# One load queue for all gate and up weights, a longer warm-up, and a new written-out order in a fused spectral and gated-linear kernel

## The chip, the cores and the metric

The kernel runs on one core of one Trainium2 chip. The metric is the device time of one execution in microseconds (us). A core has TensorE (PE, matmuls into PSUM), VectorE (DVE), ScalarE (ACT), GpSimd (POOL) and SyncE (SP, which only issues DMAs here). They run side by side and wait for each other through semaphores.

## The reference, cut to what matters

```python
def _layernorm(x, axis=-1, eps=1e-5):
    m = jnp.mean(x, axis=axis, keepdims=True)
    v = jnp.var(x, axis=axis, keepdims=True)
    return (x - m) / jnp.sqrt(v + eps)

def _A_ref(x, w_r, w_i):                      # x (1, 2048, 640)
    X = rfft2(x.astype(float32), axes=(-2, -1))
    X = X * (w_r + 1j * w_i)                  # w (2048, 321)
    return irfft2(X, s=(S, D), axes=(-2, -1)).astype(bfloat16)

def _B_ref(x, w_gate, w_up, w_down):
    g = jnp.einsum("bsd,df->bsf", x, w_gate)  # w_gate, w_up (640, 1536)
    u = jnp.einsum("bsd,df->bsf", x, w_up)
    return jnp.einsum("bsf,fd->bsd", g * u, w_down)   # w_down (1536, 640)

x = A_x
xn = _layernorm(x, axis=-1)
return x + _A_ref(xn, A_w_r, A_w_i) + _B_ref(xn, B_w_gate, B_w_up, B_w_down)
```

## The kernel before

The 2048 rows of x are split into 16 blocks of 128 rows. A block is normalised in place in SBUF, and then used by two branches that both end in the same PSUM accumulation.

The **gated branch** needs the block transposed. For blocks 0 to 3 PE transposes it (task `T0_b`, L809) and ACT or DVE copies it out of PSUM (`eT0_b`; for blocks 0 and 1 in two halves, `_act` with two of five column groups and `_dve` with three, L827). For blocks 4 to 15 SP issues a DMA transpose (`xtb`, L803), which waits for the block's normalisation. The matmuls of gate and up are the tasks `GU_f_b_u`: f is the first of twelve slabs of 128 hidden columns, b the first row block, u is 0 for gate and 1 for up. A task for four row blocks is five matmuls with 512 columns (L949, the matmul on L952); one for fewer blocks covers two slabs with ten matmuls (L969, the matmul on L974). Copies `eG` bring the results to SBUF and DVE multiplies them (`H`, L990). The down projection is the tasks `ACC_a_h_k` (L1218) per row block a, half h of the columns and group of slabs from k.

The **spectral branch** runs as a DFT by pieces: sums and differences on DVE (`S1_g` to `S5_g` per group of blocks, L854 to L895), matmuls `R_b` per block (L898) with copies `eR_b`, then `D`, `C`, the multiplication by the spectral weights (`WM`, `SM`, with copies `JA` to `JD`), and the way back (`IA`, `I`, `V1` to `V5`, and `IV`, which adds into the accumulation of the down projection). `FIN` adds x and the result is stored.

**Layer norm** of a block: either `bn` (two, L755), `ag` on DVE, or two ACT passes `sm` and `sq` (L737, L746); then `sd` (square root, ACT, L770), `rs` (reciprocal, DVE, L779) and `mul` (subtract and scale, DVE, L794). Groups of blocks share `sd` and `rs`: `sd_4` and `rs_4` serve blocks 4 and 5, `sd_5` and `rs_5` blocks 6 and 7. Blocks 0, 1, 4 and 5 use `bn`, the others ACT.

Every engine runs its tasks strictly in an order written out in `_PLAN` (L405): a tuple of task number, engine (0 PE, 1 ACT, 2 DVE, 3 POOL, 4 SP) and PSUM bank. `replay` (L151) walks the plan and `compute_waits` (L196) derives the semaphore waits from what each task reads, writes and frees; a task waits for all of these, and everything after it on its engine waits too. The durations given to tasks in the code are the planner's own; on the chip only the order, the engine, the bank and the waits of a plan count.

Loads go out as DMAs in the same way. SP issues nearly all; before, `ld_x0b` and `ld_gw0_1` go out on ACT. A load `ld_gwf_u` brings slabs from f on (two of them, 320 KB; four for f = 8, 640 KB) of gate or up (L921 to L926); `ld_xi` are pieces of x (`ld_x0a`, `ld_x0b` 80 KB each, `ld_x1` to `ld_x3` one block of 160 KB, `ld_x4` four blocks, `ld_x5` eight); `ld_sm1`, `ld_fd`, `ld_tf`, `ld_ti`, `ld_g` are DFT tables; `ld_w` spectral weights; `ld_wd` the down weights; `ld_xr` x again for the final sum. The first DVE pass over x is `S1_0`, which also waits for `mul3`; `R_0` and `R_1` need `S5_0`, and `S5_4` is what `R_12` to `R_15` need.

At the start, PE runs a **warm-up**: matmuls of ones with ones, whose result nobody reads (L712 to L719), 40 of them with 128 columns, and later a **filler** of six with 64 columns (L701 to L709), after the first transposes.

Of the kernel before, what the change touches and what calls it, by code (L numbers as in the profile page):

```python
# [400 lines left out]
def _d_act(n):  # L401
# [4 lines left out]
    (11, 4, -1), (10, 0, 5), (18, 2, -1), (12, 1, -1), (19, 2, -1), (20, 2, -1), (8, 3, -1), (0, 3, -1), (13, 4, -1),  # L406
    (28, 2, -1), (27, 2, -1), (14, 4, -1), (169, 4, -1), (15, 4, -1), (170, 1, -1), (21, 1, -1), (36, 1, -1), (22, 2, -1),
    (29, 2, -1), (30, 1, -1), (171, 4, -1), (172, 4, -1), (23, 2, -1), (24, 0, 0), (9, 0, 2), (37, 1, -1), (25, 1, -1),
    (38, 1, -1), (31, 2, -1), (32, 2, -1), (33, 0, 3), (26, 2, -1), (179, 0, 5), (39, 2, -1), (34, 2, -1), (40, 2, -1),
    (35, 2, -1), (43, 1, -1), (44, 1, -1), (45, 1, -1), (46, 2, -1), (47, 2, -1), (181, 0, 1), (182, 1, -1), (180, 1, -1),  # L410
    (183, 2, -1), (112, 2, -1), (41, 0, 7), (42, 1, -1), (189, 0, 6), (191, 0, 2), (184, 0, 0), (192, 1, -1), (190, 1, -1),
    (193, 2, -1), (48, 0, 4), (16, 4, -1), (186, 0, 1), (51, 2, -1), (50, 2, -1), (49, 1, -1), (185, 1, -1), (187, 1, -1),
    (188, 2, -1), (52, 2, -1), (54, 2, -1), (113, 2, -1), (53, 2, -1), (62, 1, -1), (63, 1, -1), (194, 0, 7), (64, 1, -1),
    (196, 0, 6), (174, 4, -1), (173, 4, -1), (55, 2, -1), (197, 1, -1), (195, 1, -1), (198, 2, -1), (114, 2, -1), (65, 1, -1),
    (204, 0, 0), (206, 0, 5), (56, 1, -1), (115, 2, -1), (57, 2, -1), (58, 2, -1), (116, 2, -1), (201, 0, 3), (205, 1, -1),
    (202, 1, -1), (66, 1, -1), (207, 1, -1), (199, 0, 2), (200, 1, -1), (208, 2, -1), (203, 2, -1), (67, 2, -1), (70, 2, -1),
    (211, 0, 1), (212, 1, -1), (17, 4, -1), (1, 4, -1), (72, 1, -1), (209, 0, 4), (117, 0, 0), (210, 1, -1), (118, 1, -1),
    (73, 1, -1), (74, 1, -1), (119, 0, 2), (121, 2, -1), (176, 4, -1), (221, 0, 7), (178, 4, -1), (175, 4, -1), (213, 2, -1),
    (216, 0, 5), (120, 1, -1), (217, 1, -1), (122, 2, -1), (68, 2, -1), (123, 2, -1), (75, 1, -1), (214, 0, 1), (215, 1, -1),
    (218, 2, -1), (124, 2, -1), (82, 1, -1), (76, 1, -1), (77, 2, -1), (125, 2, -1), (78, 2, -1), (71, 4, -1), (177, 4, -1),  # L420
    (59, 4, -1), (219, 0, 6), (60, 2, -1), (80, 2, -1), (226, 0, 4), (222, 1, -1), (220, 1, -1), (223, 2, -1), (224, 0, 0),
    (227, 1, -1), (225, 1, -1), (228, 2, -1), (130, 2, -1), (229, 0, 1), (230, 1, -1), (126, 0, 6), (127, 1, -1), (83, 1, -1),
    (128, 0, 2), (129, 1, -1), (231, 0, 0), (232, 1, -1), (233, 2, -1), (131, 2, -1), (236, 0, 4), (467, 4, -1), (237, 1, -1),
    (84, 1, -1), (85, 1, -1), (92, 1, -1), (234, 0, 5), (235, 1, -1), (238, 2, -1), (469, 4, -1), (69, 4, -1), (432, 4, -1),
    (3, 4, -1), (61, 4, -1), (86, 1, -1), (436, 4, -1), (87, 2, -1), (132, 2, -1), (241, 0, 7), (242, 1, -1), (93, 1, -1),
    (94, 1, -1), (246, 0, 2), (4, 4, -1), (431, 4, -1), (81, 4, -1), (239, 0, 3), (440, 4, -1), (240, 1, -1), (243, 2, -1),
    (244, 0, 4), (245, 1, -1), (247, 1, -1), (249, 0, 5), (251, 0, 0), (95, 1, -1), (96, 1, -1), (252, 1, -1), (250, 1, -1),
    (254, 0, 3), (255, 1, -1), (256, 0, 2), (257, 1, -1), (133, 2, -1), (248, 2, -1), (261, 0, 7), (134, 2, -1), (139, 0, 5),
    (135, 0, 0), (141, 0, 3), (97, 2, -1), (88, 2, -1), (90, 2, -1), (253, 2, -1), (266, 0, 2), (140, 1, -1), (262, 1, -1),
    (468, 4, -1), (437, 4, -1), (438, 4, -1), (472, 4, -1), (470, 4, -1), (100, 2, -1), (98, 2, -1), (258, 2, -1), (143, 2, -1),  # L430
    (142, 1, -1), (137, 0, 6), (138, 1, -1), (259, 0, 5), (260, 1, -1), (263, 2, -1), (144, 2, -1), (102, 1, -1), (267, 1, -1),
    (136, 1, -1), (264, 0, 6), (265, 1, -1), (268, 2, -1), (145, 2, -1), (269, 0, 5), (103, 1, -1), (270, 1, -1), (276, 0, 7),
    (277, 1, -1), (104, 1, -1), (271, 0, 1), (272, 1, -1), (273, 2, -1), (146, 2, -1), (274, 0, 0), (105, 1, -1), (275, 1, -1),
    (106, 1, -1), (147, 2, -1), (107, 2, -1), (281, 0, 3), (282, 1, -1), (279, 0, 7), (280, 1, -1), (284, 0, 0), (285, 1, -1),
    (286, 0, 2), (152, 0, 0), (153, 1, -1), (278, 2, -1), (473, 4, -1), (108, 2, -1), (435, 4, -1), (434, 4, -1), (466, 4, -1),
    (442, 4, -1), (439, 4, -1), (2, 4, -1), (91, 4, -1), (99, 4, -1), (154, 0, 6), (155, 1, -1), (89, 4, -1), (441, 4, -1),
    (79, 4, -1), (101, 4, -1), (110, 2, -1), (283, 2, -1), (156, 2, -1), (148, 0, 3), (149, 1, -1), (287, 1, -1), (289, 0, 5),
    (288, 2, -1), (157, 2, -1), (294, 0, 0), (295, 1, -1), (150, 0, 6), (291, 0, 1), (292, 1, -1), (290, 1, -1), (293, 2, -1),
    (296, 0, 4), (151, 1, -1), (297, 1, -1), (298, 2, -1), (301, 0, 0), (299, 0, 2), (309, 0, 1), (471, 4, -1), (109, 4, -1),
    (111, 4, -1), (433, 4, -1), (302, 1, -1), (300, 1, -1), (158, 2, -1), (7, 4, -1), (310, 1, -1), (311, 0, 3), (304, 0, 4),  # L440
    (306, 0, 5), (312, 1, -1), (307, 1, -1), (305, 1, -1), (303, 2, -1), (314, 0, 0), (159, 2, -1), (160, 2, -1), (161, 0, 1),
    (163, 0, 6), (162, 1, -1), (167, 0, 4), (168, 1, -1), (315, 2, -1), (164, 2, -1), (308, 2, -1), (313, 2, -1), (316, 0, 3),
    (317, 2, -1), (318, 2, -1), (165, 0, 6), (504, 4, -1), (502, 4, -1), (501, 4, -1), (500, 4, -1), (166, 1, -1), (321, 0, 5),
    (322, 1, -1), (443, 0, 6), (445, 2, -1), (444, 1, -1), (477, 0, 0), (446, 0, 3), (447, 1, -1), (448, 2, -1), (479, 1, -1),
    (324, 0, 2), (325, 1, -1), (478, 2, -1), (474, 0, 5), (475, 1, -1), (476, 1, -1), (449, 0, 3), (319, 0, 7), (320, 1, -1),
    (450, 2, -1), (451, 0, 1), (452, 2, -1), (453, 2, -1), (456, 3, -1), (457, 3, -1), (323, 2, -1), (455, 2, -1), (326, 0, 0),
    (327, 1, -1), (508, 0, 3), (510, 1, -1), (509, 1, -1), (331, 0, 5), (332, 1, -1), (341, 0, 7), (342, 1, -1), (505, 0, 3),
    (507, 1, -1), (506, 1, -1), (329, 0, 0), (454, 1, -1), (330, 1, -1), (482, 0, 1), (483, 2, -1), (480, 0, 5), (334, 0, 7),
    (481, 2, -1), (335, 1, -1), (349, 0, 4), (429, 4, -1), (462, 0, 3), (463, 1, -1), (536, 0, 0), (538, 1, -1), (537, 1, -1),
    (344, 0, 2), (460, 0, 3), (458, 0, 5), (350, 1, -1), (459, 1, -1), (345, 1, -1), (464, 0, 6), (465, 1, -1), (461, 1, -1),  # L450
    (336, 0, 7), (337, 1, -1), (339, 0, 0), (340, 1, -1), (328, 2, -1), (484, 2, -1), (486, 2, -1), (485, 2, -1), (503, 4, -1),
    (498, 4, -1), (497, 4, -1), (533, 4, -1), (531, 4, -1), (530, 4, -1), (499, 4, -1), (513, 0, 5), (511, 0, 3), (567, 0, 1),
    (569, 1, -1), (568, 1, -1), (346, 0, 7), (351, 0, 0), (514, 2, -1), (539, 0, 5), (512, 2, -1), (333, 2, -1), (515, 2, -1),
    (517, 2, -1), (516, 2, -1), (560, 4, -1), (487, 3, -1), (488, 3, -1), (347, 1, -1), (683, 4, -1), (528, 4, -1), (495, 0, 2),
    (541, 1, -1), (496, 1, -1), (540, 1, -1), (489, 0, 7), (490, 2, -1), (352, 1, -1), (359, 0, 1), (360, 1, -1), (493, 0, 3),
    (491, 0, 2), (492, 1, -1), (354, 0, 4), (355, 1, -1), (356, 0, 6), (494, 1, -1), (357, 1, -1), (534, 4, -1), (5, 4, -1),
    (561, 4, -1), (532, 4, -1), (535, 4, -1), (529, 4, -1), (542, 0, 1), (543, 2, -1), (366, 0, 0), (544, 0, 6), (545, 2, -1),
    (592, 4, -1), (564, 4, -1), (518, 3, -1), (565, 4, -1), (591, 4, -1), (596, 4, -1), (559, 4, -1), (563, 4, -1), (430, 4, -1),
    (601, 0, 4), (519, 3, -1), (367, 1, -1), (602, 1, -1), (603, 1, -1), (361, 0, 3), (362, 1, -1), (522, 0, 2), (523, 1, -1),
# [62 lines left out]
def _build(nc, A_x, A_w_r, A_w_i, B_w_gate, B_w_up, B_w_down, out, opts=None):  # L522
# [3 lines left out]
    with es:  # L526
# [170 lines left out]
        T("eps", "pool", 150.0, em_eps, writes=[(b_ve, None)], prio=-1.0)  # L697
        fills = []
        nfill = opts.get("nfill", 6)

        def em_fill(c):  # L701
            bk = bank_of(c.t)
            ins = None
# [642 lines left out]
```

## Time and profile before

| | |
|---|---|
| median of 3 runs | 199.5 us (198.73 to 199.68) |
| the profiled execution's own time | 199.59 us |
| its span, first to last instruction | 197.9 us |
| mean granted TensorE clock | 0.991 |
| PE busy | 192.2 us, 97% of the span |
| DVE busy | 175.4 us, 89% |
| ACT busy | 137.9 us, 70% |
| longest waits of DVE for a load of x, of PE for a gate load | 3.1 us; 0.6 us |

The span is what the profiler saw of the program; the execution's own time has 1.7 us more around it. Times in the views are counted from the start of the span. A wait in brackets is time in which the engine stood idle before an instruction, with what released it. One plan task is several instructions of a view: T0 is on L816, GU on L974 or L952, the copies on L681 (ACT) and L682 (DVE), all plain loads on L675 and DMA transposes on L804, since helpers issue them. Matmuls overlap in the views: one begins before the one before it has ended.

### The profile page before, as it was taken

The page shows a single profiled execution, that of the slowest core. Times are in us where ns is not written, and L with a number is a line of the kernel's source. Part 1 is how long each engine was busy: PE and PEld are TensorE (multiplying, and loading weights), DVE is VectorE, ACT ScalarE, POOL GpSimd, SP SyncE. Part 2 cuts the span into 40 slices and gives each one's busy share as a digit, 9 for nine tenths or more (in the row PEclk, how much of TensorE's full clock was granted, in tenths as well). Part 3 has the DMA queues.
Part 4 walks back from the last instruction along what each step waited for, and adds up shares of the span by engine and source line. Part 5 has one row for each costly group of instructions (what it writes and reads, how often), then busy time and mean ns, then how long its engine had stood idle before and what let it go on. Part 6 is the DMA issues. An engine that isn't in the chain of part 4 may idle for free.

```text
span 197.9 us, 4118 instructions
## 1 busy us (share of the span) xinstructions
PE 192.2 (97%) x1587; PEld 123.4 (62%) x1587; DVE 175.4 (89%) x364; ACT 137.9 (70%) x280; POOL 13.1 (7%) x22
## 2 busy tenths in 40 slices
PE   8699989999999999999999999999999999999995
PEld 8598735454454465556555555558677777777764
DVE  3588999999999989999999999985999999999843
ACT  3879998998976479998899998967504541440340
POOL 1000000000000000320330320330000000000000
PEclk9889999999999999999999999999999999999999
DMA  6999364979412016238492524004101252034242
GB/s 176 332 372 319 50 167 105 190 156 123 96 33 70 3 46 180 68 94 259 127 247 60 151 65 136 0 0 137 65 3 61 74 165 79 34 122 134 71 162 66
DMA packets 29666, 23.73 MB, mean 120 GB/s; under 512 B 10448, under 2 KB 27600, under 8 KB 29520
## 3 DMA queue, kind: packets, MB, share of 16 engines
q1 hardware_dynamic: 28848, 23.08, 43.8%
q10 hardware_dynamic: 800, 0.41, 0.7%
q8 instruction: 12, 0.20, 0.4%
q14 instruction: 6, 0.05, 0.1%
HBM read 18.89 MB, written 2.62 MB: 109 GB/s over the span
## 4 chain that ended last, share of the span: by engine, by line
PE 84%; DMA 7%; DVE 4%; ACT 3%; SPq 1%; issue 0%
PE ps L952 44%; PE ps L1222 25%; PE ps L1117 3%; PE ps L1035 2%; DMA arena<-in_B_w_gate_dram 2%; DMA arena<-in_B_w_down_dram 2%; PE ps L1054 2%; PE ps L1234 2%; PE ps L974 2%; DMA arena<-in_A_x_dram 2%; PE ps L906 2%; PE ps L1145 1%; ACT arena L738 1%; ACT arena L681 1%; DVE arena L797 1%; PE ps L816 1%
## 5 line engine op out<-in xcount | busy, mean ns | idle before, releaser
L681 ACT ACTIVATE arena<-ps 128x512 bf16<-128x512 f32 (+6 forms) x217 | 113.3, 579 | 50.8 <-PE ps L1234 18.0
L952 PE MATMUL ps<-arena 128*128 128x512 bf16 x420 | 97.4, 379 | 0.6 <-DMA arena<-in_B_w_gate_dram 0.6
L952 PEld LDWEIGHTS ps<-arena 128*128 128x128 bf16 x420 | 38.9, 98 | 42.1 <-DMA arena<-in_B_w_gate_dram 1.1
L1222 PE MATMUL ps<-arena 128*128 128x320 bf16 (+2 forms) x396 | 57.1, 295 | 0.2 <-DMA arena<-in_B_w_down_dram 0.2
L1222 PEld LDWEIGHTS ps<-arena 128*128 128x128 bf16 x396 | 37.4, 98 | 13.8 <-issue 0.5
L1071 DVE TENSOR_TENSOR arena<-ps,arena 128x256 bf16<-128x256 f32 x64 | 22.6, 415 | 1.9 <-PE ps L1054 1.8
L992 DVE TENSOR_TENSOR arena<-arena 128x512 bf16<-128x512 bf16 x42 | 17.9, 433 | 1.2 <-ACT arena L681 0.5
L974 PE MATMUL ps<-arena 128*128 128x128 bf16 (+1 forms) x160 | 15.3, 262 | 0.0
L974 PEld LDWEIGHTS ps<-arena 128*128 128x128 bf16 x160 | 13.7, 107 | 1.2
L682 POOL COPY arena<-arena 64x252 bf16<-64x252 bf16 x8 | 4.5, 568 | 100.7 <-DVE arena L1088 100.6
L1261 DVE TENSOR_TENSOR arena<-arena 128x640 bf16<-128x640 bf16 x15 | 7.1, 488 | 4.1 <-ACT arena L681 4.0
L747 ACT ACTIVATE arena<-arena 128x640 bf16<-128x640 bf16 x12 | 10.0, 836 | 0.1
L738 ACT ACTIVATE arena<-arena 128x640 bf16<-128x640 bf16 x12 | 8.9, 744 | 1.2 <-DMA arena<-in_A_x_dram 1.1
L1117 PEld LDWEIGHTS ps<-arena 128*128 128x128 bf16 x160 | 7.8, 116 | 2.5 <-ACT arena L681 0.2
L682 DVE CAST arena<-ps 128x320 bf16<-128x320 f32 (+3 forms) x11 | 7.0, 662 | 2.3 <-PE ps L1117 1.4
L1101 POOL TENSOR_SCALAR arena<-arena 64x252 bf16<-64x252 bf16 x8 | 7.9, 991 | 17.8 <-DVE arena L1088 17.4
L1117 PE MATMUL ps<-arena 128*128 128x64 bf16 x160 | 8.3, 198 | 0.0
L1035 PEld LDWEIGHTS ps<-arena 128*128 128x128 bf16 x160 | 6.5, 98 | 2.6 <-issue 0.3
L858 DVE TENSOR_TENSOR arena<-arena 128x768 f32<-128x768 bf16 (+1 forms) x10 | 7.9, 792 | 0.0
L1234 PE MATMUL ps<-arena 128*128 128x320 bf16 (+2 forms) x33 | 7.8, 295 | 0.0
L1035 PE MATMUL ps<-arena 128*128 128x64 bf16 (+1 forms) x160 | 7.0, 193 | 0.0
L1074 DVE TENSOR_TENSOR arena<-ps,arena 128x260 bf16<-128x260 f32 x16 | 7.0, 435 | 0.0
(61 smaller groups left out, 184.5 us busy)
## 6 DMA issues: line engine op xcount, KB each, us to landing
arena<-in_A_x_dram SPq DMA_DIRECT2D x19, 160.0 KB, 2.9
arena<-in_A_w_r_dram SPq DMA_DIRECT2D x30, 80.2 KB, 2.5
arena<-in_A_w_i_dram SPq DMA_DIRECT2D x30, 80.2 KB, 2.5
out_dram<-arena SPq DMA_DIRECT2D x15, 160.0 KB, 2.3
arena<-in_B_w_gate_dram SPq DMA_DIRECT2D x4, 320.0 KB, 6.3
arena<-in_A_x_dram SPq DMA_DIRECT2D x1, 1280.0 KB, 10.1
arena<-c_tf SPq DMA_DIRECT2D x4, 256.0 KB, 3.8
arena<-c_ti SPq DMA_DIRECT2D x2, 512.0 KB, 5.0
```

Of the source, the lines that this page charges most:

```text
L681: return c.e.activation(dst, src, _ACTF.Copy)
L682: return c.e.tensor_copy(dst, src)
L738: return c.e.activation(v_jk, v_x[:, b, :], _ACTF.Copy, scale=1.0 / _D, accum_out=v_m32[:, b:b + 1])
L747: return c.e.activation(v_jk, v_x[:, b, :], _ACTF.Square, scale=-1.0, bias=v_m32[:, b:b + 1], accum_out=v_ss[:, b:b + 1])
L952: ins = c.e.matmul(ps[:, bk, :], v_gw[:, w, j, ft, :], v_xt[:, j, rows], start=(j == 0), stop=(j == 4))
L974: ins = c.e.matmul(ps[:, bk, i * n:(i + 1) * n], v_gw[:, w, j, ft0 + i, :], v_xt[:, j, rows], start=(j == 0), stop=(j == 4))
L992: return c.e.tensor_tensor(v_ht[:, ft0, rows], gb[:, 0, :], gb[:, 1, :], _OP.mult)
L1035: ins = c.e.matmul(ps[:, bk + i, k * 64:k * 64 + n], v_uq[:, k, t + i, :], v_fd[:, k * 128 + w * n: k * 128 + w * n + n], start=True, stop ...
L1071: c.e.tensor_tensor(dst, xh, wv, _OP.mult)
L1117: ins = c.e.matmul(ps[:, bk, 64 * k:64 * k + 64], yl, v_ti[:, q, 0, :], start=True, stop=True)
L1222: ins = c.e.matmul(ps[:, bk, 0:sl3.stop - sl3.start], v_ht[:, ft, a * 128:(a + 1) * 128], v_wd[:, ft, sl3], start=(ft == _FT_ORDER[0]), st ...
L1234: return c.e.matmul(ps[:, bank_of(own), 0:sl3.stop - sl3.start], v_sm[:, 2, :], v_v[:, a, sl3], start=False, stop=True)
```

## The change

Nothing changes in what is computed. Four things change.

1. `ld_gw0_1`, the first up load, is issued by SP like the other gate and up loads, no longer by ACT.
2. The warm-up has 45 matmuls of 128 columns in place of 40, the filler five of 64 columns in place of six. `T0_1` is made to follow the filler.
3. The planner's durations of some loads, of the warm-up and of the filler are others.
4. `_PLAN` is a new order for all engines, with other PSUM banks. Eighteen tasks besides the load change between ACT and DVE: to DVE go `eT0_0_act`, `eG_0_1`, `eR_1`, `eIA_1`, `eIA_7`, `eIA_8`, `JA_9`, `eG_49_0`, `eIA_28`, `eI_0`; to ACT go `JA_3`, `eIA_4`, `JA_11`, `JA_13`, `eIA_21`, `eG_48_1`, `eIA_31`, `eI_2`.

```diff
-        nfill = opts.get("nfill", 6)
-
-        def em_fill(c):
...
-        fills.append(T("fill", "pe", opts.get("fill_ns", 53.0) * nfill, em_fill, prio=1.0, bank="single", cls="fil",
-                       selffree=True))
-        nwarm = opts.get("nwarm", 10)
+        for f_, nfill in enumerate((5,)):
+            def em_fill(c, nfill=nfill):
...
+            fills.append(T("fill%d" % f_, "pe", 42.0 * nfill, em_fill, prio=1.0, bank="single", cls="fil", selffree=True))
+        nwarm = opts.get("nwarm", 45)
 
         def em_warm(c):
             bk = bank_of(c.t)
             ins = None
-            for i in range(4 * nwarm):
+            for i in range(nwarm):
...
-        T("warm", "pe", opts.get("warm_ns", 4300.0), em_warm, prio=-1.0,
+        T("warm", "pe", opts.get("warm_ns", 107.0) * nwarm, em_warm, prio=-1.0,
...
-            dma("ld_x%d" % gi, v_x[:, b0:b0 + nb, :], xv[:, b0:b0 + nb, :], 128 * nb * (1250 if nb == 4 else 1900 if b0 == 1 else 1400 if nb == 1 else 1280),
+            dma("ld_x%d" % gi, v_x[:, b0:b0 + nb, :], xv[:, b0:b0 + nb, :], 128 * nb * (1250 if nb == 4 else 1560 if nb == 8 else 2200 if b0 == 1 else 1400 if nb == 1 else 1280),
...
-                if b == 0:
-                    for f in fills:
-                        f.deps.add(t0)
+                if b < len(fills):
+                    fills[b].deps.add(t0)
+                if 0 < b <= len(fills):
+                    t0.deps.add(fills[b - 1])
...
-                    gvs[w_][:, :, f0 * 128:(f0 + nf) * 128], 5 * 128 * nf * (480 if f0 == 6 else 340 if nf == 2 else 280),
+                    gvs[w_][:, :, f0 * 128:(f0 + nf) * 128], 5 * 128 * nf * (325 if f0 == 6 else 345 if nf == 2 else 265),
...
-                    q="act" if w_ and i < 1 else "sp")
+                    q="sp")
```

The plan itself, first part by names, since its numbers can't be read. What stands first on each engine:

```
PE before:  warm T0_0 fill T0_1 GU_0_0_0 GU_0_0_1 T0_2 GU_0_1_0 GU_0_1_1 GU_2_0_0 T0_3 GU_2_0_1 GU_2_1_0 GU_2_1_1
            GU_0_2_0 GU_0_2_1 GU_4_0_1 GU_4_0_0 GU_2_2_1 GU_2_2_0 R_0 R_1 GU_6_0_1 GU_4_2_1 GU_4_2_0 GU_6_0_0
            GU_7_0_1 GU_7_0_0 GU_8_0_0 R_2 R_3 GU_8_0_1
PE after:   warm T0_0 fill GU_0_0_1 T0_1 T0_2 GU_0_0_0 GU_0_1_1 GU_0_1_0 T0_3 GU_2_0_1 GU_2_0_0 GU_2_1_0 GU_2_1_1
            GU_0_2_1 GU_0_2_0 GU_4_0_1 GU_4_0_0 GU_2_2_0 R_1 R_0 GU_2_2_1 GU_4_2_0 GU_4_2_1 GU_6_0_1 GU_6_0_0
            GU_7_0_0 GU_7_0_1 GU_8_0_1 R_3 R_2 GU_8_0_0
ACT before: ld_x0b ld_gw0_1 sd_0 sm2 sd_1 sq2 eT0_0_act sd_2 sm3 sq3 sd_3 eG_0_1 eG_0_0 eT0_2 eG_2_1 eG_2_0 eT0_3
            eG_1_0 eG_1_1 sm6 sq6 sm7 eG_3_1 eG_3_0 sq7 sd_4 eG_5_0 eG_4_1 sd_5
ACT after:  ld_x0b sd_0 sm2 sq2 sd_1 sd_2 sm3 sq3 sd_3 eG_0_0 eT0_2 eG_2_1 eG_2_0 eT0_3 eG_1_1 eG_1_0 eG_3_0 sm6
            sq6 eG_3_1 sm7 eG_5_1 sq7 eG_4_1 sd_5 eG_5_0 sd_4
DVE before: bn0_0 bn0_1 ag0 bn1_1 bn1_0 rs_0 ag1 mul0 rs_1 mul1 eT0_0_dve rs_2 eT0_1_act mul2 eT0_1_dve rs_3 mul3
            H_0 S1_0 H_2 bn4_1 bn4_0 H_1 ag4 bn5_1 S2_0 bn5_0 ag5 H_3 S3_0 S4_0 rs_4 mul4 S5_0 H_5 H_4 rs_5 mul7
DVE after:  bn0_0 bn0_1 ag0 rs_0 mul0 bn1_1 bn1_0 ag1 eT0_0_act eT0_0_dve rs_1 rs_2 mul1 mul2 eT0_1_act eT0_1_dve
            eG_0_1 rs_3 mul3 H_0 S1_0 H_2 S2_0 H_1 bn5_0 S3_0 bn4_1 S4_0 H_3 bn4_0 bn5_1 ag5 ag4 S5_0 rs_5 rs_4 mul7
            mul4 H_4 H_5
SP before:  ld_x0a ld_x1 ld_x2 ld_gw0_0 ld_x3 ld_gw2_0 ld_gw2_1 ld_x4 ld_gw4_1 ld_gw4_0 ld_x5 ld_sm1 ld_gw6_1
            ld_gw8_1 ld_gw6_0 xt7 ld_gw8_0 xt4 ld_w2_0_1
SP after:   ld_x0a ld_x2 ld_x1 ld_gw0_1 ld_x3 ld_gw0_0 ld_sm1 ld_gw2_1 ld_gw2_0 ld_x4 ld_gw4_1 ld_gw4_0 ld_tf0
            ld_x5 ld_fd ld_gw6_1 ld_gw6_0 xt7 ld_gw8_0 xt4 ld_gw8_1 ld_w2_1_3
```

Farther on the same holds in kind: neighbouring tasks of PE change places, mostly by fewer than twenty positions of 334. Where the last `IA` tasks end, SP's order before was `ld_wd4 ld_wd6 ld_xr1 ld_xr3 ld_xr0`, and is now `ld_xr0 ld_xr3 ld_wd4 ld_xr1 ld_xr2 ld_wd6`; all of these wait for those `IA` tasks. On PE, between the last `IA` and the first task that reads what `ld_wd4` and `ld_wd6` bring (an `ACC` with k = 9), there were eleven tasks of `ACC` and `I`, before `ACC_1_1_9`, and are now sixteen, before `ACC_0_1_9`. On POOL only `JC` and `JD` of some pairs change places. The last eleven tasks of PE are the same.

## The prediction

> **What bounds the kernel now.** I read the page's busy times first, then the waits, then the start in stretches of time, then the queue of SP.
>
> ```profile
> span 197.9 us, 4118 instructions
> PE 192.2 (97%) x1587; PEld 123.4 (62%) x1587; DVE 175.4 (89%) x364; ACT 137.9 (70%) x280; POOL 13.1 (7%) x22
> ```
>
> TensorE is busy all but 5.7 us of the span. From the list of waits, the ones of PE that are no start-up:
>
> ```profile
> PEld ps L816 <- DVE arena L797: 2.0, 2, 1.3
> PE ps L816 <- DVE arena L797: 1.7, 2, 1.2
> PE ps L952 <- DMA arena<-in_B_w_gate_dram: 0.6, 1, 0.6
> PE ps L1222 <- DMA arena<-in_B_w_down_dram: 0.2, 1, 0.2
> ```
>
> So PE waits for the first layer norms, once for a gate load, once for a down load. Back-to-back matmuls overlap by 0.16 us in this view, so the last two cost 0.72 and 0.36 us; the rest of the stream from 7.44 us to 195.6 us has no hole above 0.15 us. Whatever the new order does after 30 us can only add holes. The stretches of the start, by PE, PEld, DVE, ACT, POOL and granted clock:
>
> ```profile
> 4.66:8.08 3.42, 1.68 (x26) 1.25 (x25) 1.88 (x9) 2.39 (x8) 0.00 (x0) 1.00 1.13 313
> 8.08:11.50 3.42, 3.42 (x36) 3.42 (x34) 2.26 (x9) 3.07 (x8) 0.00 (x0) 0.50 1.10 348
> 22.00:29.00 7.00, 6.44 (x41) 3.72 (x39) 7.00 (x20) 6.97 (x17) 0.00 (x0) 1.00 0.65 144
> 29.00:62.00 33.00, 33.00 (x190) 16.47 (x191) 32.39 (x60) 29.27 (x63) 0.00 (x0) 1.00 0.62 116
> ```
>
> From 8.08 to 11.50 us PE ran at half clock, after a stretch in which it was half idle. There a 128-column matmul starts every 107 ns, against 56 ns after 11.5: about 31 such starts, 1.6 us. From 22 to 62 us DVE too is 95 to 100% busy. The one gate wait, and what SP issued before it:
>
> ```profile
> 21.85 0.45 DVE L797 TENSOR_SCALAR arena<-arena 128x640 bf16<-128x640 bf16 x1
> 22.32 1.88 SPq L804 DMA_TRANSPOSE arena<-arena  x1
> 24.26 0.57 SPq L675 DMA_DIRECT2D arena<-in_B_w_gate_dram  x1
> 24.88 1.21 SPq L804 DMA_TRANSPOSE arena<-arena  x1
> 29.00 1.25 PE L952 MATMUL ps<-arena 128*128 128x512 bf16 x5 [0.56 <-DMA arena<-in_B_w_gate_dram]
> ```
>
> mul7 on DVE ends at 22.30, transpose xt7 follows, and only behind it does SP issue ld_gw8_0, which lands at 28.95 (4.70 later); GU_8_0_0 starts then.
>
> [...] ld_gw0_1 on ACT (landed 5.19) went in between SP's x1 (4.11) and x2 (5.66). [...] xt4, issued at 24.88, landed 0.62 us after ld_gw8_0, so I count what is behind a load on SP as served after it.
>
> **The change part by part.** All times are worked from durations of this one execution, span 197.9, its own time 199.59; the median of the runs is 0.09 lower.
>
> *Warm-up and filler.* Five more 128-column matmuls. The clock was full from 4.66, so they cost 5 x 56 ns and end at 5.17, ahead of T0_0 (below, 5.28): nothing, hidden by the layer norm of block 0. If they run at 107 ns the warm-up ends at 5.65 and T0_0 starts 0.37 late, which DVE's work on block 1 mostly hides. Filler: one matmul of 31 ns less.
>
> *Start order on DVE and ACT.* rs_0 and mul0 pass bn1: rs_0 starts with sd_0's end, 4.58, not 4.93; mul0 ends 5.20, not 5.57; T0_0 starts 5.28. bn1 (0.85) and ag1 run after it to 6.28, then both halves of eT0_0 on DVE (0.55). GU_0_0_1 starts at 6.93; before, PE's stream began at 7.44. x2, now second on SP, lets ACT take sm2 at 4.6 instead of 5.69, so sd_1 and sd_2 are done by 6.8. DVE goes on with rs_1, rs_2, mul1, mul2 (to 7.92), eT0_1 when T0_1 is done (8.65), eG_0_1 0.30, rs_3 and mul3 0.57: 9.52. Then, in start-to-start times of the trace: H_0 0.25, S1_0 1.61, H_2 0.25, S2_0 1.20, H_1 0.25, bn 0.44, S3_0 1.46, bn 0.44, S4_0 0.68, H_3 0.25, two bn 0.88, two ag 0.30, S5_0 0.66, in all 8.67: 18.19. rs_5, rs_4, mul7 0.76: mul7 ends at 18.95, 3.35 earlier than before. Of this 2.2 is DVE idle time from 8 to 21 us that is gone, 0.7 is H_4 and H_5 now behind mul7.
>
> *PE at full clock.* GU_0_0_1 0.56, T0_1 at 7.62 (mul1), T0_2 at 7.98 (mul2), three 10 x 128 groups, T0_3 0.28: 10.22. Four groups of GU_2 2.24: 12.46. Five groups of 10 x 256 at 1.09: 17.91. R_1 waits for S5_0: 18.27; R_1, R_0 0.56; three more 1.09: 22.10; GU_6 and GU_7, four at 1.08: 26.42. Here GU_8_0_1 is next. By then PE has done just what it had done at 29.00 before.
>
> *Loads.* ld_gw0_1 behind x2 and x1 lands when 800 KB are in: 5.7, as before for 800 KB; wanted at 6.93. x1 as third lands near 4.7; DVE wants it at 5.20. sm1, tf0 and fd (480 KB) pass ahead of gw6, gw8_1 (640 KB) goes behind: gw6_1 near 20.4, gw6_0 near 20.9 at the 0.3 MB/us of the trace (x5: 1280 KB in 4.25 us), wanted at 22.1 and 23.2. These cost nothing; the cover of gw6 is 1.7 us.
>
> *ld_gw8_1* is the exception. It stood ahead of xt7 and landed at 20.7. Now SP holds xt7, ld_gw8_0, xt4, ld_gw8_1, and GU_8_0_1, which reads it, stands ahead of R_3, R_2 and GU_8_0_0. xt7 issues at 19.0 and takes 1.2 (the other transposes) to 1.9 (this one before). ld_gw8_0 at 20.25 to 20.95 lands 4.7 later, xt4 0.62 behind, then 640 KB at 0.3: 27.7 to 28.4. If it needs only a load's own 4.7 from its issue (22.15 to 22.85): 26.9 to 27.5. So GU_8_0_1 starts between 26.95 and 28.45; I take 27.75[...]. PE stalls 1.3 us, twice what it did before, and is 1.25 ahead of before.
>
> *Later.* The down load: SP puts x residual loads ahead of wd4 and wd6, all waiting for the last IA, at 134.65 in before's time. wd6 issues near 137.2; with 4.5 (as before) it lands at 141.7; PE has 7.1 us of work first, 141.75. The hole of 0.36 becomes 0 to 0.4: I count no gain. Eighteen tasks change between ACT and DVE, most near equal (320 columns 0.44 and 0.48); JA takes 1.05 on ACT and 0.50 on DVE, three go to ACT, one comes back. GU groups on PE cover 0.55 each; uncovered, 1.1 net. POOL only swaps pairs.
>
> Sum: 199.59 - 1.25 = 198.34; less 0.09: 198.3.
>
> **The rivals.** *The whole lead is kept.* ld_gw8_1 lands before 26.4: 2.58, and the down hole 0.36: 196.7 at best, 197.0 taken. For it: the floor of PE allows it. Against: 19.0 plus four issues and two 640 KB loads.
>
> *The clock falls anyway.* [...] With half clock from 8.08, GU_0_1 and then H_2, H_1, sm6, sq7, sd_4 come late and mul7 ends at about 20.0: the load lands 27.9 to 29.5, PE starts near 28.8, gain 0.2: 199.3.
>
> *Slower: xt7 is held by the loads ahead.* SP's queue drains until 20.9, and before xt7 was issued into an empty queue; ld_gw6_0's issue, into a full one, took 2.42 us. Issued in effect at 20.9 (1.9 later) and landing like xt11, with loads in flight (4.73 against 2.98, 1.75 more), it puts ld_gw8_1 at 30.6 to 32.1: PE 2.3 behind, 201.8. It decides from a landing past 30.0. Against: 1.75 need not come on top.
>
> **How the numbers follow.** Stopped by the load with a lead, 0.5, its own range 197.4 to 199.0. Whole lead 0.2, clock 0.17, held transpose 0.13. 0.5% is 1.0 us, about what a measurement of this kernel can tell from no change: faster is below 198.5. Faster: two thirds of the first, and the second, 0.53; slower: the last and a little of the clock, 0.15; 0.32 within. The range goes from the whole lead, 196.8, to the clock case with a further hole, 200.1; it leaves out the held transpose and the far floor.
>
> **What would show it.** Right: PE's stream starts near 6.9; no stretch at 0.50 after 5 us; xt7 issued near 19; one wait of L952 for the up load, 0.5 to 2 us near 27 to 28, and no other above 0.4. Wrong: that wait gone or above 3 us; half clock; R_1 later than 19; DVE's S5_4 late at 69 us, where it had only 0.27 us to spare before R_12; new holes at C, IA or the down projection.

## The result and the profile after

The changed kernel takes 201.58 us, median of four runs (200.73 to 202.25), against 199.51 us before; the ratio is 1.0109 with a 95% interval of 1.0062 to 1.0156. It is slower by about 2 us, and outside the range that was predicted. The page of the changed kernel begins:

```profile
span 199.9 us, 4124 instructions
PE 192.9 (97%) x1591; PEld 123.2 (62%) x1591; DVE 176.0 (88%) x366; ACT 139.1 (70%) x278; POOL 12.9 (6%) x22
```

The span has grown by 2.0 us, PE's busy time by 0.7. The waits of PE in the changed kernel that answer to those shown of before (L973 was L974, L951 was L952):

```profile
PEld ps L951 <- DMA arena<-in_B_w_up_dram: 3.2, 1, 3.2
PE ps L951 <- DMA arena<-in_B_w_up_dram: 2.8, 1, 2.8
PE ps L973 <- DVE arena L778: 0.8, 1, 0.8
```

The short wait for a gate load has turned into a long one for an up load. The waits for the first layer norms have shrunk from 1.7 to 0.8 us. SP's queue, the load's time in flight from the chain of waits, and PE around the wait:

```profile
18.33 1.56 SPq L802 DMA_TRANSPOSE arena<-arena  x1
19.95 0.57 SPq L675 DMA_DIRECT2D arena<-in_B_w_gate_dram  x1
20.57 1.21 SPq L802 DMA_TRANSPOSE arena<-arena  x1
21.82 0.58 SPq L675 DMA_DIRECT2D arena<-in_B_w_up_dram  x1
```

```profile
21.82 7.08 DMA arena<-in_B_w_up_dram
```

```profile
28.95 2.18 PE L951 MATMUL ps<-arena 128*128 128x512 bf16 x5 [2.75 <-DMA arena<-in_B_w_up_dram]
30.92 1.27 PE L905 MATMUL ps<-arena 128*128 128x128 bf16 x10
31.98 2.38 PE L951 MATMUL ps<-arena 128*128 128x512 bf16 x9
```

The four lines of SP are xt7, ld_gw8_0, xt4 and ld_gw8_1. ld_gw8_1 is issued at 21.82 and lands at 28.90, so GU_8_0_1 starts at 28.95. With the 0.16 us by which the view lets matmuls overlap, the wait of 2.75 is a hole of 2.91 us. And look at the length of the group behind the hole: five matmuls of 512 columns in 2.18 us, where before the change a group of the same shape, the one at 29.00, took 1.25. The stretches show why; columns are the stretch, PE, PEld, DVE, ACT, POOL and the granted clock:

```profile
5.23:29.12 23.89, 20.37 (x222) 16.26 (x220) 23.34 (x69) 21.94 (x56) 0.00 (x0) 1.00 0.98 280
29.12:32.53 3.41, 3.41 (x17) 1.92 (x16) 2.33 (x4) 0.30 (x1) 0.00 (x0) 0.50 0.60 133
32.53:62.00 29.47, 29.47 (x168) 14.58 (x167) 26.30 (x48) 26.29 (x58) 0.00 (x0) 1.00 0.29 70
```

For 3.41 us behind the hole PE runs at half clock. The half clock of 8.1 to 11.5 us, which the kernel before had, is gone from the start:

```profile
4.66:8.08 3.42, 2.65 (x43) 2.47 (x42) 3.14 (x13) 3.32 (x9) 0.00 (x0) 1.00 1.09 321
8.08:11.50 3.42, 3.42 (x64) 3.39 (x62) 3.18 (x11) 3.25 (x10) 0.00 (x0) 1.00 1.07 329
```

So the account by places, in the two profiled executions. When PE comes to slab 8 it has done the same work in both; it starts on it at 28.95 in place of 29.00: nearly the whole lead of the start is used up by the wait. Once both groups of slab 8 and R_2, R_3 are done, the next group starts at 33.34. In the kernel before it starts at 31.72, since the group ahead of it begins at 30.64 and takes 1.08:

```profile
30.64 0.59 PE L952 MATMUL ps<-arena 128*128 128x512 bf16 x2
```

The changed kernel is 1.6 us behind here. That is 3.41 us at half clock, in which half of the work, 1.7 us, was not done, less the 0.05 of lead. At the end, IV_15_2 starts at 197.37, and before at 195.36: it is 2.0 behind. The other 0.4 are small holes from C_0 (77 us) to ACC_13_0_0 (186 us): six of 0.06 to 0.34 us, 1.0 in all, where the kernel before has 0.6 us of such holes, 0.36 of them for the down load, which is gone.

### The profile page after: what moved, and what is told of

It is laid out like the page before. It is cut to its first block, busy times and chain, and to the rows that moved or that the text cites. A ratio compares the mean times of both kernels' runs of the same rounds, so it can differ in the third digit from the quotient of the medians.

```text
span 199.9 us, 4124 instructions
## 1 busy us (share of the span) xinstructions
PE 192.9 (97%) x1591; PEld 123.2 (62%) x1591; DVE 176.0 (88%) x366; ACT 139.1 (70%) x278; POOL 12.9 (6%) x22
## 4 chain that ended last, share of the span: by engine, by line
PE 74%; DVE 13%; DMA 8%; SPq 1%; ACT 1%; issue 1%; DVEq 0%
PE ps L951 44%; PE ps L1221 17%; DMA arena<-in_B_w_up_dram 4%; PE ps L1116 3%; PE ps L1034 2%; PE ps L1053 2%; PE ps L905 2%; DMA out_dram<-arena 2%; DMA arena<-in_A_x_dram 2%; PE ps L1144 2%; PE ps L1233 1%; SPq L675 1%; DVE arena L991 1%; DVE arena L1260 1%; DVE arena L857 1%
## 5 line engine op out<-in xcount | busy, mean ns | idle before, releaser
L951 PE MATMUL ps<-arena 128*128 128x512 bf16 x420 | 99.0, 382 | 2.8 <-DMA arena<-in_B_w_up_dram 2.8
L951 PEld LDWEIGHTS ps<-arena 128*128 128x128 bf16 x420 | 39.2, 98 | 44.1 <-DMA arena<-in_B_w_up_dram 3.2
L1221 PEld LDWEIGHTS ps<-arena 128*128 128x128 bf16 x396 | 37.5, 98 | 13.8 <-ACT arena L681 0.5
L1100 POOL TENSOR_SCALAR arena<-arena 64x252 bf16<-64x252 bf16 x8 | 8.4, 1044 | 107.9 <-DVE arena L1087 107.7
L973 PE MATMUL ps<-arena 128*128 128x128 bf16 (+1 forms) x160 | 13.9, 246 | 0.8 <-DVE arena L778 0.8
L973 PEld LDWEIGHTS ps<-arena 128*128 128x128 bf16 x160 | 12.2, 98 | 1.9 <-DMA arena<-in_B_w_up_dram 0.9
L682 DVE CAST arena<-ps 128x320 bf16<-128x320 f32 (+4 forms) x14 | 8.9, 647 | 2.0 <-PE ps L1116 0.9
L1116 PEld LDWEIGHTS ps<-arena 128*128 128x128 bf16 x160 | 7.8, 116 | 3.0 <-issue 0.5
L1034 PEld LDWEIGHTS ps<-arena 128*128 128x128 bf16 x160 | 6.5, 98 | 2.6 <-ACT arena L681 0.5
L905 PEld LDWEIGHTS ps<-arena 128*128 128x128 bf16 x80 | 5.7, 104 | 2.7 <-issue 0.8
```

The lines of the kernel that those rows point to most:

```text
L905: ins = c.e.matmul(psflat[:, bk * 512 + k * 128: bk * 512 + (k + 1) * 128], st, v_sm[:, 1, :], start=True, stop=True)
L951: ins = c.e.matmul(ps[:, bk, :], v_gw[:, w, j, ft, :], v_xt[:, j, rows], start=(j == 0), stop=(j == 4))
L973: ins = c.e.matmul(ps[:, bk, i * n:(i + 1) * n], v_gw[:, w, j, ft0 + i, :], v_xt[:, j, rows], start=(j == 0), stop=(j == 4))
L1034: ins = c.e.matmul(ps[:, bk + i, k * 64:k * 64 + n], v_uq[:, k, t + i, :], v_fd[:, k * 128 + w * n: k * 128 + w * n + n], start=True, stop ...
L1116: ins = c.e.matmul(ps[:, bk, 64 * k:64 * k + 64], yl, v_ti[:, q, 0, :], start=True, stop=True)
L1221: ins = c.e.matmul(ps[:, bk, 0:sl3.stop - sl3.start], v_ht[:, ft, a * 128:(a + 1) * 128], v_wd[:, ft, sl3], start=(ft == _FT_ORDER[0]), st ...
```

## The experiments

**Theory:** the loss is the wait of GU_8_0_1 for a load that stands on SP behind two transposes, and the half clock that this hole brings. **Rival:** the new order is slower elsewhere, and the wait only stands where another engine would have been late anyway. Each of the first three runs takes away one piece; the fourth puts the cause into the kernel before.

The edits of order are shown by task names. A time is the median of a run's executions; the ratio to the kernel before on the same chip need not be the quotient of two medians. Waits and timelines come from one profiled execution, which is not always near the median.

**The load ahead of the transposes** (a1_load_ahead):

```diff
-SP: ld_gw6_1 ld_gw6_0 xt7 ld_gw8_0 xt4 ld_gw8_1
+SP: ld_gw6_1 ld_gw6_0 ld_gw8_1 xt7 ld_gw8_0 xt4
```

> The changed kernel with one load moved on SP: the second up load of slabs 8 to 11 (ld_gw8_1) goes out right behind ld_gw6_0, ahead of transpose xt7, as it did before the change. Theory (the loss is the wait of GU_8_0_1 for this load, 2.9 us, and the half clock that follows it, 1.7 us): the load lands near 23.2, PE does not wait, no stretch at 0.50 after the start, 201.6 - 4.6 = 197.0 us, between 196.5 and 198. Rival (the new order is slower elsewhere, the wait only uses up time that DVE would cost anyway): PE waits at R_3, R_2 or later instead, 200 us or more.

Measured: 197.32 us against 199.15 of before on the same chip, ratio 0.9912 (0.9871 to 0.9953). PE around slab 8 in this run:

```profile
24.66 2.97 PE L962 MATMUL ps<-arena 128*128 128x512 bf16 x13
27.46 0.72 PE L916 MATMUL ps<-arena 128*128 128x128 bf16 x10
28.02 6.21 PE L962 MATMUL ps<-arena 128*128 128x512 bf16 x28
```

There is no hole; the load landed at 23.34 and GU_8_0_1 began at 26.39. Moving one load on SP's queue turns 1.1% slower into 0.9% faster, near the expected 197.0. DVE, which the rival names, was hardly in the way: its last S5 ends at 67.10 and holds R_15, the first task that needs it, for 0.11 us.

The 0.9% over before have two parts. The mean clock that is listed with each execution is 1.0 at full clock throughout and 0.991 with one stretch of 3.41 us at half. All six executions of this run had 1.0. Of the 33 of the kernel before, 18 had 0.991, with a median of 199.45 us, and 15 had 1.0, with 197.97. Between executions of full clock the gain is 0.65 us; the rest is the half clock that the kernel before has in about half of its executions.

**The gate group first** (a2_gate_first), loads as in the changed kernel:

```diff
-PE: GU_7_0_1 GU_8_0_1 R_3 R_2 GU_8_0_0
+PE: GU_7_0_1 GU_8_0_0 GU_8_0_1 R_3 R_2
```

> The changed kernel with GU_8_0_0 ahead of GU_8_0_1 on PE; loads as they are. The gate load has landed, so PE has 1.08 us of work before it waits for the same load: a hole of 1.8 us in place of 2.9. If a hole of 1.8 us keeps the clock: 201.6 - 1.1 - 1.7 = 198.8 us. If it still halves the clock: 200.5 us. Rival (order elsewhere): 201.6.

Measured: 199.12 us, ratio 1.0005 (0.9978 to 1.0032), so level with before.

```profile
30.14 1.25 PE L962 MATMUL ps<-arena 128*128 128x512 bf16 x5 [1.70 <-DMA arena<-in_B_w_up_dram]
31.23 0.72 PE L916 MATMUL ps<-arena 128*128 128x128 bf16 x10
```

The hole is 1.86 us and the five matmuls behind it take 1.25: the clock was kept, as the mean clock of all twelve executions says too. By the medians the run is 2.5 us faster than the changed kernel, about twice the 1.1 us by which the hole became shorter. (The profiled execution, 200.23 us, is the slowest of the twelve; its xt7 was issued 1.3 us later than in the changed kernel.)

**PE kept busy in the hole** (a3_keep_clock): 48 matmuls of ones, whose result nobody reads, ahead of GU_8_0_1; the loads stay as they are.

```diff
+        keep = T("keep", "pe", 48 * 56.0, em_keep, bank="single", cls="fil", selffree=True)
-PE: GU_7_0_1 GU_8_0_1 R_3 R_2 GU_8_0_0
+PE: GU_7_0_1 keep GU_8_0_1 R_3 R_2 GU_8_0_0
```

> The changed kernel with 48 matmuls of ones of 128 columns ahead of GU_8_0_1 on PE (2.7 us at full clock), whose result nobody reads; the wait for the load stays. Theory: the hole halves the clock, and with PE busy in it the clock stays full: 201.6 - 1.7 = 199.9 us, GU_8_0_1 still starts near 28.9. Rival (the half clock has another cause): still a stretch of 3.4 us at 0.50, 201.6 us.

Measured: 199.83 us, ratio 1.0054 (1.003 to 1.0077).

```profile
26.05 2.98 PE L1270 MATMUL ps<-const-bfloat16-1.0 128*128 128x128 bf16 x48
28.87 1.24 PE L951 MATMUL ps<-arena 128*128 128x512 bf16 x5
```

GU_8_0_1 starts as late as in the changed kernel, at 28.87. In this execution it is the 48 matmuls that hold it so long: the load had landed at 28.14. Its five matmuls take 1.24 us, and from 29.0 to 32.4 the clock is full:

```profile
29.00:32.40 3.40, 3.40 (x25) 1.83 (x23) 2.46 (x4) 1.70 (x3) 0.00 (x0) 1.00 0.55 125
```

Useless work in the hole brings the time near the 199.9 expected, and all twenty executions kept the clock (mean clock 0.999 or 1.0). So the half clock is a cost of its own, and here it comes from PE's idleness. Its size is 1.7 us by the account above; by these runs it is 1.8 us between the medians and 1.1 us between the two ratios to before, whose intervals overlap a little.

**The cause put into the kernel before** (a4_load_last):

```diff
-SP: ld_gw6_1 ld_gw8_1 ld_gw6_0 xt7 ld_gw8_0 xt4 ld_w2_0_1
+SP: ld_gw6_1 ld_gw6_0 xt7 ld_gw8_0 xt4 ld_gw8_1 ld_w2_0_1
-PE: GU_7_0_0 GU_8_0_0 R_2 R_3 GU_8_0_1
+PE: GU_7_0_0 GU_8_0_1 GU_8_0_0 R_2 R_3
```

> The kernel before with the suspected cause put in and nothing else of the change: ld_gw8_1 behind xt4 on SP, and GU_8_0_1 ahead of GU_8_0_0 on PE. xt7 is issued at 22.3 as before; the load lands some 10.6 us later as in the changed kernel, 32.9. Theory: PE waits 4.5 us there in place of 0.7 and then runs 3.4 us at half clock, 199.5 + 3.9 + 1.7 = 205.1 us. If the wait alone counts: 203.4. Rival (the order elsewhere is the cause): near 199.5.

Measured: 205.68 us, ratio 1.031 (1.0258 to 1.0362). PE's timeline at slab 8, as far as the view reaches, has the hole, 4.2 us long:

```profile
31.05 3.17 PE L964 MATMUL ps<-arena 128*128 128x512 bf16 x7 [4.04 <-DMA arena<-in_B_w_up_dram]
```

The stretch behind it shows the clock in the last column but two, at 0.50:

```profile
31.00:36.00 5.00, 4.96 (x17) 2.20 (x18) 1.39 (x2) 0.47 (x1) 0.00 (x0) 0.50 0.80 154
```

Nothing else of the change is in this kernel, and it loses 3.1%, about 6 us. Here the half clock lasted 6.8 us (29.5 to 36.3), and PE had work from 31.05 on. A hole that is 3.5 us longer than the one before, and half of the 5.3 us behind it, make 6.1. With that and the first run the rival has fallen.

The next four ask which parts of the change are worth something. They share a median of 199.71 us of before. Of its 62 executions, 21 had the full clock throughout (median 198.5 us) and 41 one stretch at half (199.8).

**Warm-up and filler alone** (b1_warm_alone), on the kernel before:

```diff
-        nfill = opts.get("nfill", 6)
+        nfill = opts.get("nfill", 5)
-            for i in range(4 * nwarm):
+            for i in range(45):
```

> The kernel before with the warm-up of 45 and the filler of 5 alone. PE is then busy to about 5.4 us instead of 4.9 and the hole ahead of T0_0 is closed. If this keeps the half clock of 8.1 to 11.5 us away in most executions: up to 1 us faster, near 198.2 us. If the hole from 6.2 to 7.4 us is what counts, as before: 199.2 us, no change.

Measured: 198.61 us, ratio 0.9969 (0.9938 to 1.0001): inconclusive, perhaps a little faster. Twelve of the twenty executions had the full clock, against 21 of 62, which could still be chance. The profiled execution had its half clock:

```profile
5.15:8.56 3.41, 1.83 (x29) 1.40 (x27) 1.89 (x9) 2.56 (x8) 0.00 (x0) 1.00 1.16 319
8.56:11.97 3.41, 3.41 (x36) 3.41 (x34) 2.34 (x9) 2.85 (x8) 0.00 (x0) 0.50 1.09 343
```

**The queue alone** (b2_queue_alone), on the kernel before:

```diff
-                    q="act" if w_ and i < 1 else "sp")
+                    q="sp")
-ACT: ld_x0b ld_gw0_1 sd_0       SP: ld_x0a ld_x1 ld_x2 ld_gw0_0
+ACT: ld_x0b sd_0                SP: ld_x0a ld_x1 ld_x2 ld_gw0_1 ld_gw0_0
```

> The kernel before with ld_gw0_1 on SP behind ld_x2 and nothing else. [...] the load lands some 0.5 us later, at 5.7 to 6.3, and is wanted at 8.7: no change, 199.2 us. If the second queue had brought bandwidth: later loads all land later, PE's wait for the gate load of 8 grows, over 200 us.

Measured: 198.01 us, ratio 0.9947 (0.9922 to 0.9972). Both expectations missed: it is faster. PE's start in this run, and then three lines of the kernel before (L816 there is L827 here):

```profile
5.67 0.45 PE L827 MATMUL ps<-arena 128*128 128x128 bf16 x5 [0.40 <-DVE arena L808]
6.74 0.45 PE L827 MATMUL ps<-arena 128*128 128x128 bf16 x5 [0.43 <-DVE arena L808]
```

```profile
5.69 0.74 ACT L738 ACTIVATE arena<-arena 128x640 bf16<-128x640 bf16 x1 [1.11 <-DMA arena<-in_A_x_dram]
6.73 0.17 DVE L780 RECIPROCAL arena<-arena 128x1 f32<-128x1 f32 x1 [1.16 <-ACT arena L773]
7.44 0.45 PE L816 MATMUL ps<-arena 128*128 128x128 bf16 x5 [1.17 <-DVE arena L797]
```

T0_1 starts at 6.74, and 7.44 before. The way there leads over x2. On ACT, sm2 waits for x2, sd_1 stands behind sm2, and rs_1 on DVE (the RECIPROCAL) waits for sd_1. With the up load gone from in between, x2 lands at 4.96 in place of 5.66, rs_1 starts at 6.03 in place of 6.73, and block 1 is normalised 0.7 us sooner. (x1 lands sooner too, 3.60 for 4.11, but DVE's pass over it starts at 4.22, and before at 4.17.) The hole at the start is shorter, and the clock stayed full in this execution and in 18 of the 20. That is most of the gain: between executions of full clock 0.6 us are left.

**The first fix with the old warm-up** (b3_ahead_old_warm): the order of a1_load_ahead, and

```diff
-        for f_, nfill in enumerate((5,)):
+        for f_, nfill in enumerate((6,)):
-        nwarm = opts.get("nwarm", 45)
+        nwarm = opts.get("nwarm", 40)
```

> The changed kernel with ld_gw8_1 ahead of xt7, as in the first run, and the old warm-up of 40 and filler of 6. If the new start order alone keeps the clock full: 197.3 us as with 45 and 5. If the longer warm-up is what keeps it: some executions show 3.4 us at half clock near 8 us, median 198 to 199 us.

Measured: 198.1 us, ratio 0.9919 (0.9891 to 0.9947), against 0.9912 of a1_load_ahead: the longer warm-up is worth nothing that these runs can tell, once the start order is the new one. The profiled execution has no half clock before its end, and ten of the eleven executions had the full clock.

**The gate load ahead, in the kernel before** (b4_gate_load_ahead):

```diff
-SP: ld_gw6_1 ld_gw8_1 ld_gw6_0 xt7 ld_gw8_0 xt4
+SP: ld_gw6_1 ld_gw8_1 ld_gw6_0 ld_gw8_0 xt7 xt4
```

> The kernel before with one load moved: ld_gw8_0 right behind ld_gw6_0, ahead of xt7. It lands near 23.7 and PE's one gate wait of 0.7 us is gone: 0.5 to 0.7 us faster, 198.5 us. If DVE, busy all through 22 to 62 us, is what sets R_2 to R_15: the gain is lost again by 70 us, 199.2 us.

Measured: 198.72 us, ratio 0.9968 (0.9938 to 0.9998): a small gain, just clear of no change. The gate wait is gone: GU_8_0_0 begins at 28.73 without a hole, 0.27 us sooner, though the holes at this execution's start were 0.36 us longer. IV_15_2 begins at 194.86 in place of 195.36, so on balance nothing of it is lost again later. The kernel before had the same fault as the changed one, a load behind a transpose, only smaller.

**Two moves** (c1_two_moves): a1_load_ahead, and

```diff
-PE: IV_12_1 ACC_13_0_0 ACC_13_0_5 ACC_13_0_9 ACC_12_0_5 ACC_12_0_9
+PE: IV_12_1 ACC_12_0_5 ACC_12_0_9 ACC_13_0_0 ACC_13_0_5 ACC_13_0_9
```

> The changed kernel with ld_gw8_1 ahead of xt7 as in the first run, and the three tasks ACC_13_0 behind ACC_12_0_9 on PE. In the first run PE waited 0.74 us at ACC_13_0_0 for a copy on ACT that waited for a store. With 0.95 us of other work first the hole is gone: 197.3 - 0.5 = 196.8 us. If the wait only moves on to the next task that needs a bank: 197.3 us.

Measured: 197.18 us (197.03 to 197.35), against 199.4 of before, ratio 0.9895 (0.9852 to 0.9939). In the profile the hole at ACC_13_0_0 is gone and no other has come; the time can't be told from that of a1_load_ahead, whose interval holds it. Both beat both kernels.

**The load between** (c2_ahead_of_xt4):

```diff
-SP: xt7 ld_gw8_0 xt4 ld_gw8_1
+SP: xt7 ld_gw8_0 ld_gw8_1 xt4
```

> The changed kernel with ld_gw8_1 ahead of xt4 but still behind xt7 and ld_gw8_0. [...] it lands 2.1 us behind ld_gw8_0, near 27.3; the hole ahead of GU_8_0_1 is 1.3 us and keeps the clock: 201.6 - 1.6 - 1.7 = 198.3 us. If one engine of the sixteen lags as in the changed kernel, it lands near 28.3, the hole is 2.3 us: 201.0 with half clock, 199.3 without.

Measured: 198.86 us, ratio 0.9992 (0.9963 to 1.002), again against 199.4. By the ratios this is 2.3 us faster than the changed kernel, and between the two cases that were expected. PE's timeline:

```profile
29.29 1.25 PE L962 MATMUL ps<-arena 128*128 128x512 bf16 x5 [2.59 <-DMA arena<-in_B_w_up_dram]
```

In this execution the load lands no sooner for standing ahead of xt4: at 29.25, 10.3 us behind xt7's issue, where the changed kernel had 10.6. But the execution took 200.0 us and is one of the slowest of the twenty, which go down to 197.22 with the full clock in all of them. The others must have waited less; when their load landed is not on record. So these runs do not show how much xt4 itself held the load up. What they show is why a load can come later than its place in the queue says. The stretches of that time, of which the last two columns are the DMA share and GB/s:

```profile
26.00:27.00 1.00, 0.70 (x4) 0.10 (x1) 1.00 (x5) 1.00 (x3) 0.00 (x0) 1.00 3.07 73
27.00:28.00 1.00, 0.00 (x0) 0.00 (x0) 1.00 (x5) 1.00 (x4) 0.00 (x0) 1.00 0.07 25
28.00:29.00 1.00, 0.00 (x0) 0.00 (x0) 1.00 (x4) 0.56 (x2) 0.00 (x0) 1.00 0.07 23
```

For two whole us the share is 0.07, about one DMA engine of sixteen, moving 23 to 25 GB/s. The changed kernel shows the same tail:

```profile
26.00:27.00 1.00, 0.20 (x1) 0.00 (x0) 1.00 (x4) 1.00 (x4) 0.00 (x0) 1.00 1.06 335
27.00:28.00 1.00, 0.00 (x0) 0.00 (x0) 1.00 (x4) 1.00 (x3) 0.00 (x0) 1.00 0.07 24
```

The trace records the completion of a load in sixteen parts, and the load has landed when the sixteenth is in. Of ld_gw8_1 in the changed kernel, fifteen parts were in at 27.63 and the last at 28.90. Of ld_gw8_0 in this run, fifteen were in at 25.02 and the last at 27.43.

Why one part lags is open. It happens elsewhere too: in a4_load_last the last two parts of ld_gw8_1 came 0.7 and 0.8 us behind the others, in a1_load_ahead the last of xt4 1.5 us. One candidate is the queue that the page of the changed kernel lists as instruction (q8: 12 packets, 0.20 MB). A single packet of 16 KB on it, which takes 1.0 us, starts at 25.07 in the changed kernel and one at 26.16 in a1_load_ahead, while the late transfer is in flight; in the kernel before it starts at 22.59, ahead of ld_gw8_0's issue, and no part of that load lags. The two late parts in a4_load_last had no such packet beside them. None of this was tried apart.

## Why the prediction was wrong

**Right.** The start: GU_0_0_1 at 6.80 (predicted 6.93), mul7 done at 18.30 (18.95), xt7 issued at 18.33 (19.0), PE at GU_8_0_1 at 26.04 (26.42), no half clock at the start. The place of the new wait, the load, the queue order behind it, and "one wait of L952 for the up load", were named before the run; the down hole is gone, as allowed. The rival that the clock falls at the start did not come about in this execution.

**Wrong: the price of the hole.** This is the step that failed. "PE stalls 1.3 us" was entered at its length, and what the hole does to the clock was put at nothing. The runs show a hole of 2.91 us and 3.41 us at half clock behind it, which cost another 1.7 us. a3_keep_clock takes off only the second, a1_load_ahead both. The prediction had seen 3.42 us at half clock at the start of the kernel before, behind a stretch of 3.42 us with PE busy for 1.68, and did not put the same question to the hole that it forecast itself. A hole of 1.3 us would probably have been harmless; that is an estimate from a2_gate_first, which kept the clock with one of 1.86 us. The upper end of its own range, 2 us, stands just above that. One execution of the four of the changed kernel has a mean clock of 1.0; it is the fastest, at 200.73 us, 0.8 to 1.5 below the other three, and still slower than before.

**Wrong too: the landing of ld_gw8_1.** The step took 27.75, from a range of 26.95 to 28.45. It landed at 28.90 though xt7 had gone out 0.7 us earlier than predicted: 10.6 us from xt7's issue to the landing, where the step's own terms gave 7.9 to 9.4. ld_gw8_0 (5.24 from its issue, priced at 4.7) and xt4 (0.64 behind it, priced at 0.62) came nearly as priced. The last term, 2.1 us for 640 KB, was 3.07. Fifteen of the sixteen parts of the load were in at 27.63, near the 27.75; the last came 1.27 us later, and nothing in the prediction stands for that. PE was there 0.4 us sooner and the load 1.2 us later, and so the hole was 2.9 us, not 1.3.

**Right in number, not in cause: the rival on the slower side.** It gave 201.8 for a transpose held back by the loads ahead. xt7 was not held: it was issued in 1.56 us as soon as mul7 was done and landed 3.3 us later. The lateness was in the load, and the rest of the loss in the clock. So this number is no confirmation.

**Sized at nothing, and not nothing:** moving ld_gw0_1 off ACT's queue. The prediction put its own landing against its first use and found no cost. b2_queue_alone gains 0.5%: what counts is that x2 is no longer delayed by it. The direction could have been read from landings that the prediction itself gives: in the kernel before this load landed at 5.19, and x2 only behind it, at 5.66. In b2_queue_alone, with the load behind x2 on SP, x2 landed at 4.96.

In hindsight the sum is this: the 1.25 us of lead become 0.05, the half clock costs 1.7, and small holes 0.4, so that 199.59 - 0.05 + 1.7 + 0.4 = 201.6, the time of the profiled execution. Of the 3.3 us that were missing, 1.2 are the load's landing, 1.7 the clock and 0.4 the holes.

## What to carry to other kernels

A load that stands in SP's order behind a DMA that waits for another engine inherits that engine's time: ld_gw8_1 landed at 28.90 behind the transposes and at 23.34 ahead of them (a1_load_ahead). Put behind them in the kernel before, it made a hole of 4.2 us (a4_load_last); with ld_gw8_0 ahead of them, the wait of 0.56 us was gone (b4_gate_load_ahead). Look for each such pair and put the load in front. Price a hole on PE twice: by its length, and by the half clock that can follow it, which here cost 1.7 us on top of 2.9. Where the hole stayed, useless work moved into it (a3_keep_clock, 48 matmuls of ones) or a ready task put ahead of it (a2_gate_first, 1.86 us in place of 2.91) saved the clock. When executions of one kernel fall into two groups of clock, compare within a group before you credit a change with the difference.

## What the runs showed of the hardware

The half clock of TensorE came in stretches of 3.4 us (before, 8.08 to 11.50; after, 29.12 to 32.53; b1_warm_alone, 8.56 to 11.97) and once of 6.8 us (a4_load_last, 29.5 to 36.3). For five profiled executions the table has PE's hole ahead of a group of slab 8, or the work in its place, and the clock behind it:

| execution | PE's hole | clock behind it |
|---|---|---|
| a4_load_last | 4.20 us | half, from 29.5, inside the hole, to 36.3 |
| changed kernel | 2.91 us | half, for 3.41 us |
| c2_ahead_of_xt4 | 2.75 us | full; mean clock of the execution 1.0 |
| a2_gate_first | 1.86 us | full; mean clock of the execution 1.0 |
| a3_keep_clock | none, 48 matmuls of ones in 2.98 us | full from 29.0 to 32.4 |

So a long hole on PE can be followed by half clock, and one nearly as long need not be: 2.91 us against 2.75 is one execution each. From which length on, and what else decides, was not shown.

The kernel before had the half clock in some executions and not in others: 18 of 33 on one chip, 1.5 us slower by the medians, and 41 of 62 on another, 1.3 us slower. Why an execution falls into the one group or the other was not shown.
